# Moving the later wq loads and the last wq-gradient store to Pool's DMA queue, in the backward pass of a decode block with attention over a cache

## The chip, the cores and the metric

The kernel runs on one core of a Trainium2 chip. The metric is the device time of one execution in microseconds (us); lower is better. A core has five engines with instruction streams of their own: PE (matmul), DVE (vector), ACT (scalar), POOL (GpSimd) and SP (which here only issues transfers). SP, ACT and POOL issue the DMA transfers. All transfers are moved by the core's 16 DMA engines; the profile names the queues q1 (issued by SP), q10 (by ACT) and q0 (by POOL, with descriptors made in software).

## The reference, cut to what matters

One token attends with 32 heads over caches of 8192 positions, beside a gated MLP. Wanted are the output and the gradients of all inputs but one. The caches and their gradients are the bulk of the traffic: 32 heads x (K, V, dK, dV) of 2 MiB each.

```python
def _A_ref(x, k_cache, v_cache, wq, wo):
    q = (x @ wq).reshape(B, Sq, Hq, Dh).transpose(0, 2, 1, 3)
    scores = jnp.einsum("bhqd,bhkd->bhqk", q, k) * (Dh ** -0.5)
    p = _softmax(scores, axis=-1)
    o = jnp.einsum("bhqk,bhkd->bhqd", p, v)
    return o.transpose(0, 2, 1, 3).reshape(B, Sq, Hq * Dh) @ wo

x = A_x
xn = _layernorm(x, axis=-1)
return x + _A_ref(xn, A_k_cache, A_v_cache, A_wq, A_wo) + _B_ref(xn, B_w1, B_w3, B_w2)
...
_out, _vjp = jax.vjp(_f, A_x, A_k_cache, A_v_cache, A_wq, A_wo, B_w1, B_w3, B_w2)
_grads = _vjp(grad_out)
```

With one query, dV of a head is the outer product of the probabilities and the gradient of o, dK the outer product of the score gradients and q, and the gradient of wq is the outer product of xn and dq. wq is 640 x 4096 in bf16.

## The kernel before, in words

The order of the instructions on each engine is the order of the program text (a manual schedule). The MLP comes first (some 45 us), then one pass of the loop at L725 per head, then the last head written out from L779.

In a pass, head `h` gets its probabilities (`probs`), its dV in two halves (`outer` with "V"), its score gradients (`dscores`) and its dK in two halves (`outer` with "K"), while the score products of head `h + 1` are made (`product`, L414 on DVE and L416 on PE). `outer` writes into a 2 MiB tile `ot` (L430 on ACT, L436 on DVE) from a pool of four, and after the second half POOL stores it (L443). The last two heads are stored in halves by SP (L441). K tiles come from a pool of three, V tiles from one of two; SP issues their loads (L115 and L122) as soon as a tile is free.

wq is kept in two buffers of 8 heads (`wq_bufs`, 1280 KB each): block `b`, heads `8b` to `8b + 7`, lies in buffer `b % 2`. Blocks 0 and 1 are loaded at the start. When a block's heads are done, ACT writes the block's wq gradient into the same buffer (L372) and POOL stores it (`store_columns`, L141), in columns 0 to 2 and 3 to 4 of the five that each partition holds; `sparing` cuts these stores into 120 and 8 rows, and `turn_lanes` (L137) puts tiny loads into a `lane_pad` between them, which move on the DMA engine at which the next one starts. Only after that may the buffer take block `b + 2`. So just two loads are issued inside the loop, block 2 and block 3, and `WQ_AT` (L718) says where: the key is the head's number within the running block and one of three places in the pass (0 after dV's second half, 1 after the wo load, 2 after dK's second half), the value is the first column, the number of columns and the queue (SP where none is named). Before, ACT loads columns 0 to 2 during the block's third head (heads 10 and 18), and SP one column each at places 0 and 2 of the fourth (heads 11 and 19).

The first reader of block 2 is `prep_steps(4)`, whose first step (the matmuls into `ps_q`, L311) runs in the first `gap` of head 14; for block 3 that is head 22. PE runs it in order, so that all that follows on PE would wait for a late wq.

At the end, the gradient of the last four heads' wq columns is made in the tile `dwq_t` (L802) and stored by ACT (L804); behind it on ACT stands the store of the output (`fin_bf`, L841). SP stores the last wo gradient (L807) and the gradient of x (`dx_bf`, L836). POOL's last transfers are three stores kept back until head 29 (`late`, L767: wq gradient of block 2, a wo gradient, the wq gradient of group 6) and a `lane_pad`.

Of the kernel before, what the change touches and what calls it, by code (L numbers as in the profile page):

```python
# [21 lines left out]
def kernel(  # L22
# [22 lines left out]
    nc = tc.nc  # L45
    H = A_k_cache.shape[1]
    SK = A_k_cache.shape[2]
    DH = A_k_cache.shape[3]
# [7 lines left out]
    GH = 4  # L56
# [36 lines left out]
    dwq_v = out_4.rearrange("(p ci) n -> p ci n", ci=NC)  # L93
# [9 lines left out]
    with tc.manual_schedule(engines=ORDERED):  # L103
# [65 lines left out]
        def load_wq(b, c0=0, n=NC, by=nc.sync.dma_start):  # L169
            wq_g = wq_bufs[b % 2]  # L170
            part, src, _ = wq_part(b, c0, n)
            by(part, src)
            for g in range(b * HB, (b + 1) * HB):
                c0 = (g - b * HB) * GH * DH
                grp.setdefault(g, dict(wq_all=wq_g, wq=wq_g[:, :, c0:c0 + GH * DH]))
# [539 lines left out]
        exps(first)  # L715
        product(first, "DP", 1)
        prev = None
        WQ_AT = {(2, 1): (0, 3, nc.scalar.dma_start), (3, 0): (3, 1), (3, 2): (4, 1)}  # L718

        def wq_columns(h, part):  # L720
            b, r = divmod(h, GW)
            if 0 < b < H // GW - 1 and (r, part) in WQ_AT:
                load_wq(b + 1, *WQ_AT[r, part])

        for h in range(H - 1):  # L725
            n = new_head(h + 1) if h + 1 < H else None
            c = hs.pop(h)
            g, hh = divmod(h, GH)
# [51 lines left out]
        g = c.g  # L780
# [19 lines left out]
        dwq_t = tpool.tile([P, NC, GH * DH], BF16, name="dwq_t", tag="T")  # L800
        for ci in range(NC):
            nc.scalar.activation(dwq_t[:, ci, :], c.G["dqbc"][:].rearrange("p h d -> p (h d)"),  # L802
                                 ACTF.Copy, scale=xn_col[:, ci:ci + 1])
        nc.scalar.dma_start(dwq_v[:, :, g * GH * DH:(g + 1) * GH * DH], dwq_t[:])  # L804
        for r in range(GH):
            nc.vector.tensor_scalar(c.G["wo"][:, r, :], g_bc_bf[:], on[:, r:r + 1], None, ALU.mult)
        nc.sync.dma_start(dwo_v[g], c.G["wo"][:])  # L807
# [64 lines left out]
```

## Time and profile before

| | |
|---|---|
| median of 3 runs | 720.65 us (719.62 to 720.72) |
| the profiled execution | 720.15 us, of it 718.4 us span |
| moved | 303.32 MB, mean 422 GB/s |
| busy | DVE 631.4 us, PE 555.2, ACT 479.3, POOL 49.5 |
| packets q1 / q0 / q10 | 13490 / 10960 / 3196 |
| wq loads inside the loop | ACT at 269.4 and 436.8 us; SP at 286.8, 290.7, 453.8, 456.9 us |
| first use of the new wq blocks (L311) | 351.4 and 516.1 us |
| last store of wq's gradient (L804) | issued at 703.9 us, landed 13.3 us later |

"Span" is the time from the first to the last instruction of the profiled execution. Times in the text are on the span's clock. A DMA's landing is the moment when its semaphore has been counted up by all 16 engines. Not only instructions but every DMA packet (queue, size, start, duration) is in the trace; the queue table of the profile is summed from these.

### The profile page before, as it was taken

How to read it: one execution, taken by the hardware profiler on the slowest of the kernel's cores; microseconds unless marked ns; L12 is line 12 of the kernel's file. 1: busy time of each engine (PE TensorE's matmuls, PEld its weight loads, DVE VectorE, ACT ScalarE, POOL GpSimd, SP SyncE). 2: the span in 40 equal slices, each digit the busy share in tenths (PEclk: the TensorE clock that was granted, in tenths of full speed). 3: DMA queues.
4: the chain of work that ended last, by engine and by line, in shares of the span. 5: the costliest groups of instructions: out<-in, count | busy, mean ns of one | idle time of the engine just before them, and what ended most of it. 6: DMA issues, size and time to landing. Idle time of an engine off the chain costs nothing.

```text
span 718.4 us, 9840 instructions
## 1 busy us (share of the span) xinstructions
PE 555.2 (77%) x3516; PEld 274.3 (38%) x3516; DVE 631.4 (88%) x723; ACT 479.3 (67%) x1456; POOL 49.5 (7%) x91
## 2 busy tenths in 40 slices
PE   5787788888788786775888788497877888888862
PEld 3653343333344333332443344143433334333331
DVE  5789999999999996896799999499999989899992
ACT  2165677696779756695487866469677857678551
POOL 0010000000001210000000110000000000000100
PEclk9699989999998988997799979779899889999995
DMA  8999999999999999999999999999999999999997
GB/s 351 415 426 424 431 430 401 430 429 428 434 428 430 430 425 424 425 427 428 430 426 432 430 427 422 428 428 429 429 429 431 430 428 433 427 430 431 428 422 304
DMA packets 27694, 303.32 MB, mean 422 GB/s; under 512 B 3264, under 2 KB 3974, under 8 KB 9982
## 3 DMA queue, kind: packets, MB, share of 16 engines
q1 hardware_dynamic: 13490, 154.89, 51.0%
q0 software_dynamic: 10960, 137.72, 45.1%
q10 hardware_dynamic: 3196, 10.10, 3.5%
q8 instruction: 27, 0.44, 0.2%
q14 instruction: 21, 0.17, 0.1%
HBM read 151.34 MB, written 151.34 MB: 421 GB/s over the span
## 4 chain that ended last, share of the span: by engine, by line
DVE 41%; DMA 36%; PE 15%; ACT 5%; issue 1%; SPq 0%; POOL 0%; DVEq 0%; ACTq 0%; POOLq 0%
DMA Kt<-in_A_k_cache_dram 20%; DVE T L414 19%; DVE ot L436 12%; DMA out_dram<-ot 10%; DMA lane_pad<-in_A_wq_dram 4%; PE ob L485 4%; PE psDP L416 4%; ACT ot L430 3%; PE psS L416 3%; DMA dbc<-in_B_w_dram 2%; DVE S_sb L457 1%; DVE DP_sb L511 1%; PE ps_od L501 1%; PE dx_ps L612 1%; DVE P L476 1%
## 5 line engine op out<-in xcount | busy, mean ns | idle before, releaser
L416 PE MATMUL psDP<-T,ident_bf 128*128 128x512 bf16 x512 | 158.1, 465 | 67.4 <-DVE T L414 67.2
L416 PEld LDWEIGHTS <-ident_bf 128*128 128x128 bf16 x1024 | 107.9, 109 | 205.3 <-issue 131.1
L430 ACT ACTIVATE ot<-qs_g,Uf 128x128 bf16<-128x128 bf16 x496 | 151.7, 394 | 43.5 <-DVE Uf L523 26.5
L414 DVE TENSOR_TENSOR T<-Kt,qs_g 128x4096 bf16<-128x4096 bf16 x64 | 146.4, 2287 | 14.9 <-DMA Kt<-in_A_k_cache_dram 13.7
L430 ACT ACTIVATE ot<-do_g,Pf 128x128 bf16<-128x128 bf16 x504 | 154.0, 389 | 7.0 <-DMA out_dram<-ot 6.0
L414 DVE TENSOR_TENSOR T<-Vt,do_g 128x4096 bf16<-128x4096 bf16 x64 | 146.0, 2282 | 5.6 <-DMA Vt<-in_A_v_cache_dram 5.6
L416 PE MATMUL psS<-T,ident_bf 128*128 128x512 bf16 x512 | 126.4, 391 | 10.0 <-DVE T L414 10.0
L436 DVE TENSOR_TENSOR ot<-qs_g,U 128x3072 bf16<-128x3072 bf16 (+1 forms) x64 | 113.2, 1768 | 12.4 <-DMA out_dram<-ot 12.3
L436 DVE TENSOR_TENSOR ot<-do_g,P 128x3072 bf16<-128x3072 bf16 (+1 forms) x64 | 112.9, 1764 | 7.1 <-DMA out_dram<-ot 6.1
L443 POOL DMA_DIRECT2D out_dram<-ot x60 | 32.2, 536 | 548.4 <-DVE Uf L523 315.1
L485 PE MATMUL ob<-Vt,P 128*4 128x512 bf16 x512 | 62.2, 386 | 0.0
L485 PE MATMUL ob<-Kt,U 128*4 128x512 bf16 x512 | 60.5, 379 | 1.3 <-DVE U L518 1.3
L478 ACT ACTIVATE Pf<-E,rZ 128x16 f32<-128x16 f32 x32 | 9.7, 304 | 57.9 <-DVE rZ L474 57.9
L542 ACT ACTIVATE dq_diag<-ident_bf,odq 128x128 bf16<-128x128 bf16 x32 | 12.8, 401 | 50.9 <-DVE odq L538 50.9
L501 PEld LDWEIGHTS ps_od<-pick,wide 128*128 128x128 f32 x256 | 42.2, 233 | 8.3 <-issue 2.8
L501 PE MATMUL ps_od<-pick,wide 128*128 128x2 f32 x256 | 37.2, 267 | 0.5 <-ACT wide L493 0.5
L461 PE MATMUL sm<-ident_f,mrow 128*128 128x128 f32 x64 | 15.9, 331 | 24.1 <-DVE mrow L459 24.1
L485 PEld LDWEIGHTS <-U 128*4 128x4 bf16 x512 | 19.8, 84 | 37.4 <-DVE U L518 6.9
L485 PEld LDWEIGHTS <-P 128*4 128x4 bf16 x512 | 20.6, 85 | 24.7 <-issue 1.5
L493 ACT COPY wide<-ob 128x256 f32<-128x256 f32 x64 | 20.0, 362 | 10.5 <-PE ob L485 10.5
L306 ACT COPY woT<-ps_t 128x512 bf16<-128x512 bf16 x40 | 23.0, 576 | 5.2 <-PE ps_t L301 4.5
L457 DVE TENSOR_REDUCE S_sb<-psS 128x64 f32<-128x512 f32 x32 | 21.9, 685 | 4.5 <-PE psS L416 4.5
(173 smaller groups left out, 549.9 us busy)
## 6 DMA issues: line engine op xcount, KB each, us to landing
out_dram<-ot POOLq DMA_DIRECT2D x60, 2048.0 KB, 24.1
Kt<-in_A_k_cache_dram SPq DMA_DIRECT2D x32, 2048.0 KB, 26.5
Vt<-in_A_v_cache_dram SPq DMA_DIRECT2D x32, 2048.0 KB, 20.5
out_dram<-ot SPq DMA_DIRECT2D x8, 1024.0 KB, 13.3
out_dram<-wo_g ACTq DMA_DIRECT2D x6, 640.0 KB, 15.2
wo_g<-in_A_wo_dram ACTq DMA_DIRECT2D x6, 640.0 KB, 15.6
wq<-in_A_wq_dram SPq DMA_DIRECT2D x2, 1280.0 KB, 33.7
w1t<-in_B_w_dram SPq DMA_DIRECT2D x1, 2160.0 KB, 12.7
```

Of the source, the lines that this page charges most:

```text
L306: nc.scalar.copy(woT[:], ps_t[:])
L414: nc.vector.tensor_tensor(T[:], src[:, :, ds_], vec[:, ds_].unsqueeze(1).to_broadcast([P, J, DHH]), ALU.mult)
L416: nc.tensor.matmul(ps[:], lhsT=ident_bf[:], rhs=T[:, :, RUN * i:RUN * (i + 1)], start=(half == 0 and i == 0), stop=(half == 1 and i == DHH ...
L430: nc.scalar.activation(st.ot[half][:, JH - ACT_J + j].rearrange("p a b -> p (a b)"), vec, ACTF.Copy, scale=wf[:, half, j:j + 1])
L436: nc.vector.tensor_tensor(st.ot[half][:, 0:n], vec.rearrange("p (a b) -> p a b", b=2).unsqueeze(1).to_broadcast([P, n, DH // 2, 2]), w2[:, ...
L443: nc.gpsimd.dma_start(dst.rearrange("p j d -> p (j d)"), st.rows[:])
L457: nc.vector.tensor_reduce(st.S[:], st.ps["S"][:], AX.X, ALU.add)
L461: nc.tensor.matmul(st.sm[:, 8:8 + P], lhsT=mrow[:].to_broadcast([P, P]), rhs=ident_f[:], start=True, stop=True, skip_group_check=True)
L485: nc.tensor.matmul(ob[c0:c0 + WIDE, :], lhsT=w2[:, WIDE * q:WIDE * (q + 1), 0], rhs=src[:, WIDE * q:WIDE * (q + 1), :].rearrange("p j d -> ...
L493: nc.scalar.copy(part[:], ob[:, i * (WIDE // 2) * DH:(i + 1) * (WIDE // 2) * DH])
L501: nc.tensor.matmul(st.od, lhsT=st.wide[i][:, b * DH:(b + 1) * DH], rhs=pick[:, r, :], start=(r == 0), stop=(r == WIDE - 1), skip_group_che ...
L542: nc.scalar.activation(dq_diag[:], ident_bf[:], ACTF.Copy, scale=odq[:, 1:2])
```

## The change

Two lines change. The wq loads inside the loop are both issued by POOL, at places 0 and 2 of the block's fourth head (heads 11 and 19): columns 0 to 2 directly behind the store of dV, columns 3 and 4 directly behind the store of dK. The store of `dwq_t` is issued by POOL too.

```diff
-        WQ_AT = {(2, 1): (0, 3, nc.scalar.dma_start), (3, 0): (3, 1), (3, 2): (4, 1)}
+        WQ_AT = {(3, 0): (0, 3, nc.gpsimd.dma_start), (3, 2): (3, 2, nc.gpsimd.dma_start)}
...
-        nc.scalar.dma_start(dwq_v[:, :, g * GH * DH:(g + 1) * GH * DH], dwq_t[:])
+        nc.gpsimd.dma_start(dwq_v[:, :, g * GH * DH:(g + 1) * GH * DH], dwq_t[:])
```

In the built program ACT loses three DMA instructions, SP four, POOL gains five; PE's and DVE's orders stay as they were, and no compute instruction changes. No byte is added or taken away.

## The prediction

> **What bounds the kernel now.** I read the slices first, then the stretches of 18 us, the queue table, DVE's waits, and last the end of the timeline. The page (span, slices, queues) has these lines:
>
> ```profile
> span 718.4 us, 9840 instructions
> ...
> DVE  5789999999999996896799999499999989899992
> ...
> DMA  8999999999999999999999999999999999999997
> GB/s 351 415 426 424 431 430 401 430 429 428 434 428 430 430 425 424 425 427 428 430 426 432 430 427 422 428 428 429 429 429 431 430 428 433 427 430 431 428 422 304
> ...
> q1 hardware_dynamic: 13490, 154.89, 51.0%
> q0 software_dynamic: 10960, 137.72, 45.1%
> q10 hardware_dynamic: 3196, 10.10, 3.5%
> ```
>
> The reader is to see that the DMA engines are full in every slice but the first and the last, while DVE has a hole (the 4 at 450 us). The three queues' shares add up to 99.6%. Four stretches, with their columns (busy us of each engine, granted clock, DMA share, GB/s):
>
> ```profile
> core 0: us, PE busy (x) PEld busy (x) DVE busy (x) ACT busy (x) POOL busy (x), PEclk, DMA share, GB/s
> ...
> 270.00:288.00 18.00, 12.75 (x68) 5.71 (x69) 10.47 (x14) 12.16 (x36) 1.06 (x2) 0.81 1.02 425
> ...
> 324.00:342.00 18.00, 9.84 (x54) 4.65 (x50) 11.74 (x11) 8.27 (x28) 1.06 (x2) 0.75 1.00 424
> ...
> 450.00:468.00 18.00, 7.54 (x52) 3.34 (x52) 8.03 (x9) 8.93 (x28) 0.53 (x1) 0.76 1.01 425
> ...
> 684.00:702.00 18.00, 12.09 (x95) 6.64 (x94) 16.54 (x20) 10.45 (x34) 0.00 (x0) 0.99 1.01 422
> ```
>
> DVE works 8 of 18 us in one of them and the DMA engines carry as much as ever. So a compute stall in the loop is the effect of the full DMA engines, and taking one away moves it elsewhere. What DVE waits for there:
>
> ```profile
> DVE ot L436 <- DMA out_dram<-ot: 18.4, 4, 9.9
> DVE T L414 <- DMA Kt<-in_A_k_cache_dram: 13.7, 10, 3.7
> DVE T L414 <- DMA Vt<-in_A_v_cache_dram: 5.6, 1, 5.6
> ```
>
> Stores that free an `ot` tile too late, then loads. The time is therefore the sum of what the packets cost on the slowest DMA engine, plus a start and an end. The end, from the timeline:
>
> ```profile
> 702.84 0.43 SPq L807 DMA_DIRECT2D out_dram<-wo_g  x1
> ...
> 703.89 0.62 ACTq L804 DMA_DIRECT2D out_dram<-dwq_t  x1
> ...
> 708.10 0.33 SPq L836 DMA_DIRECT2D out_dram<-dx_bf  x1
> 708.29 0.30 ACTq L841 DMA_DIRECT2D out_dram<-fin_bf  x1
> ```
>
> By the trace's landing records, POOL's kept-back stores are drained at 708.9, the wo gradient lands at 716.6, `dwq_t` at 717.2 (its first engine at 710.7, the middle one at 714.8), `dx_bf` at 717.0 and `fin_bf`, behind `dwq_t` on q10, at 717.4. DMA engines with work in hand, not the 708.3 of the last issue, set the end.
>
> **The change, part by part.** *Price of the packets.* In the packet records SP's and ACT's wq loads are packets of 2 KB at 86.6 ns mean: 2 blocks x 128 rows x 5 columns = 1280 packets, 110.8 us, over 16 engines 6.93 us. POOL's stores of the same buffers were packets of 4 KB: q0 holds 1112 of them at 160.0 ns, and 1112 x 4 KB is the 4480 KB of wq gradient that POOL stores, all but 32 KB. If POOL's loads are packed alike, they are 640 x 160.0 ns / 16 = 6.40 us: -0.53. `dwq_t` by ACT is 640 packets of 1 KB at 46.1 ns, 1.84 us; by POOL 160 x 160.0 / 16 = 1.60: -0.24. No row shows POOL loading wq, so the bounds: 2 KB packets that stay so, 0; the dearest row per KB (46.1 ns for 1 KB), 2560 KB x 46.1 / 16 = 7.37, +0.44. I take -0.53, since the nearest rows, the stores of the same tiles by the same queue, are packed.
>
> *Issue.* A POOL DMA takes 0.54 us (60 `ot` stores), up to 1.02 for 640 pieces (the last L767). Five more are 4 us on an engine busy 49.5 of 718: nothing on the path. Behind each stands only the next store; the dK store of head 11 follows its neighbour by 9.4 us. ACT loses a 4.2 us wait ahead of its load at 269.4 (L172's semaphore instruction, 4157 ns), in a stretch where DVE waits for stores anyway: 0.
>
> *Waits of the loads.* In the built program a POOL DMA waits for the landing of the eighth before it. For block 2 these are head 9's dV store (landed 279.5) and the 120-row gradient store (283.3); the loads' places are behind the stores at 286.6 and 296.0. For block 3: 445.7 and 453.7 against 452.8 and 469.7. All over before: 0. If the cover were gone, the next dK store would wait with them, and four `ot` tiles later DVE.
>
> *Who is delayed now.* On one engine q0 and q1 take turns packet by packet: between 256.5 and 259.5 us q0 moved 71 packets of 4 KB beside 61 of 16 KB on q1. The Trainium skill (DMA: Bandwidth & Descriptors, "Queues, rings and completion order") has the engines switch only after a whole packet of some 9 to 17 descriptors; by the 71 to 61 the trace does not agree for these 16 KB rows. By the rule each of POOL's 20 small packets of a block would stand behind a row block of 8 x 0.611 us, 20 x (0.160 + 4.9) = 101 us from 286.6 and 452.8, so that L311 would wait 36 and 38 us and the time come near 790; the rows leave it a chance of 0.01.
>
> By turns of single packets SP's 2 KB packets cost the loads turns: 8 per engine and part, 16 x (0.087 + 0.611 of a 16 KB store packet) = 11.2 us per block; DVE's 5.6 us wait for V at 329 and the 3.7 for K at 343 follow. After, 12 + 8 packets of 4 KB cost the stores 20 x (0.160 + 0.611) = 15.4 us per block, and what is late next is an `ot` tile two heads on. The DMA engines stay full meanwhile, since loads run ahead: 0 on the path. That cover ends if compute is more than 5.0 us later at the end: `dwq_t` is issued at 703.9 and q0 drains at 708.9.
>
> *Landing of wq.* Before, head 11's dK store landed at 321.0 and head 19's at 493.8. With the first part's 12 turns (9.3 us) and the second's 8 (6.2) on top, wq lands near 336 and 509; L311 needs it at 351.4 and 516.1. Hidden, with 15 and 7 us; without the cover PE waits, and DVE behind it.
>
> *End.* `dwq_t` comes into q0 behind 708.9 on the last engine, its 10 packets among SP's last; `fin_bf` is alone on q10. The last landing goes from 717.4 to between that and `dx_bf`'s 717.0: -0.4 to 0, I take -0.2.
>
> Sum: -0.53 - 0.24 - 0.2 = -0.97. The profiled execution, 718.4 span and 1.75 around it, would go from 720.15 to 719.2. It was 0.5 below the median, so I forecast 719.7.
>
> **The rivals.** *Stores too late (slower).* The 15.4 us fall on the stores, and four `ot` tiles cover less than K's and V's five. For it: the stretch at 450 us, where POOL's small gradient packets had just this effect (the 9.9 us wait). Against it: such a wait cost no DMA time there. It decides when the lateness outlives the ten heads behind head 19; a second wait of 9.9 us, less the 5.0 of cover, gives +4.9: 720.65 + 4.9 - 0.8 for the packets = 724.8; with half of the lateness forgotten by then, 722.3.
>
> *More than the packets (faster).* The engines finish 6.5 us apart (710.7 to 717.2, the middle at 714.8). If the lag comes from the hardware queues' small pieces, moving them levels it: up to -2.4 beside the -0.97, 717.3. For it: no other row explains the lag. Against: both queues spread 128 rows over the engines evenly.
>
> *The transfer is hidden anyway (no change).* POOL's loads stay at 2 KB and the end is SP's: 0, 720.65. The Trainium skill (the same page, "Issuing engines are not separate DMA queues") says that spreading issues only saves issue time; by that rule this is the outcome. Against: the 4 KB rows.
>
> **How the numbers follow.** Forecast 0.55, own range 718.4 to 721.2 (the packets' bounds and the 1.1 us between the three runs); stores too late 0.20; levelled 0.13; no change 0.11; the skill's long packets 0.01. The range 717.4 to 723.0 leaves out most of the worst half of the slow case and the tail of the levelled one. Faster or slower means by over 0.2% (1.44 us), about what a measurement of this kernel can tell: the forecast puts 0.18 of its 0.55 below 719.2 and 0.02 above 722.1; with 0.13 of levelling, faster is 0.31. The slow case gives 0.17 of its 0.20, with the 0.02 and the 0.01 slower is 0.20; the rest, 0.49, is no change that can be told.
>
> **What would show it.** q10 falls from 10.10 to 7.9 MB, q0 rises to 141, and q0's packets by 800 and 16 semaphore writes for each of five transfers, some 880 and not 2000. DVE's waits for K and V at 329 to 347 shrink, and waits for `ot` appear at heads 13 and 21. L311 does not start late. The DMA share stays at 1.00 to 1.02 from 270 to 700. I am wrong if a stretch after 290 falls below 0.98, if L804 lands last, or if the time leaves 718.4 to 721.2.

## The result, and the profile after

The changed kernel takes 722.38 us (median of 20 runs, 719.56 to 725.3), the kernel before beside it 719.74 (20 runs, 719.05 to 721.71): a ratio of 1.0027, interval 1.0017 to 1.0038. It is slower by 0.27%, some 1.9 us. The ratio on record isn't the quotient of the two medians, which lie 2.64 us apart (1.0037); where this text gives microseconds from medians, the ratio beside them is the safer number. The time lies in the range of 717.4 to 723.0; the forecast said 719.7 and gave most weight to no change that can be told, so the direction was missed. The profiled execution took 722.25 us.

The page after (span, slices, queues):

```profile
span 720.5 us, 9824 instructions
...
GB/s 358 409 422 428 431 429 428 431 429 429 428 432 429 426 427 424 420 424 425 432 428 429 429 426 424 422 419 429 430 426 431 426 431 428 429 432 428 429 421 260
...
q1 hardware_dynamic: 12914, 153.84, 50.5%
q0 software_dynamic: 11840, 141.00, 46.2%
q10 hardware_dynamic: 1740, 7.87, 2.6%
```

The queues moved as foretold: q0 has 880 packets more. Of DVE's waits:

```profile
DVE ot L436 <- DMA out_dram<-ot: 35.2, 8, 7.7
DVE T L414 <- DMA Kt<-in_A_k_cache_dram: 6.2, 7, 1.7
```

K's waits fell from 13.7 to 6.2 us, V's are gone, those for `ot` rose from 18.4 to 35.2. The swap was foretold. What was not is seen in the stretches beside the wq loads (columns as before the prediction). Before:

```profile
288.00:306.00 18.00, 13.66 (x94) 6.12 (x93) 16.75 (x18) 11.93 (x42) 0.53 (x1) 0.91 1.01 427
306.00:324.00 18.00, 14.19 (x80) 6.50 (x80) 17.42 (x20) 16.59 (x47) 1.06 (x2) 0.91 1.01 425
...
468.00:486.00 18.00, 17.36 (x102) 8.14 (x101) 16.63 (x20) 11.12 (x35) 1.07 (x2) 0.77 1.01 430
```

After:

```profile
288.00:306.00 18.00, 15.95 (x106) 7.25 (x104) 16.85 (x20) 11.94 (x40) 1.28 (x2) 0.91 1.01 421
306.00:324.00 18.00, 13.28 (x86) 6.35 (x85) 17.75 (x19) 16.72 (x49) 1.09 (x2) 1.00 1.01 421
...
468.00:486.00 18.00, 13.65 (x102) 6.59 (x100) 17.75 (x18) 14.90 (x47) 1.09 (x2) 1.00 1.00 417
```

The share of the DMA engines (the last column but one) is 1.00 to 1.01 in all six, and yet 4 to 13 GB/s are missing after. A share counts how long packets are under way; it doesn't say that they are as short as they could be.

The packet records give the account. For packets that start between 265 and 650 us (before the first changed load and up to the loop's last heads), summed and divided by the 16 engines:

| us | before | after | difference |
|---|---|---|---|
| small packets (2 to 8 KB) | 24.17 | 23.76 | -0.41 |
| 16 KB packets, what they took above 611.3 ns each | 1.65 | 3.16 | +1.51 |
| tiny packets and semaphore writes | 1.16 | 1.04 | -0.12 |
| less overlap of packets | 3.40 | 3.04 | +0.36 |
| sum | | | +1.34 |

611.3 ns is what nearly every 16 KB packet takes. "Less overlap" is the time by which the packets of all engines together exceed 385 us per engine: packets of one engine overlap a little, and after they do so less. The bytes agree: 164.90 MB before and 164.32 after in the same stretch, 0.58 MB or 1.36 us at 428 GB/s. Of the 1.51 us of long packets 1.34 lie where the wq loads are (265 to 335 and 440 to 545 us), with packets of up to 1253 ns in the first of these stretches and 1886 in the second (before 1258 and 1144). The saving in small packets was right; it is paid for more than three times over by the large packets around them.

The other part is the end. The timeline after:

```profile
708.33 0.86 POOL L804 DMA_DIRECT2D out_dram<-dwq_t  x1 [37.04 <-issue]
...
710.64 0.33 SPq L836 DMA_DIRECT2D out_dram<-dx_bf  x1
710.83 0.29 ACTq L841 DMA_DIRECT2D out_dram<-fin_bf  x1
```

In this execution `dwq_t` left 4.4 us later than before: 2.2 because ACT's last write of it came later (706.08; the granted clock was 0.72 from 684 to 702 us, 0.99 before), and 2.2 between that write and POOL's issue. The last landings were 718.58 (`dwq_t`), 718.99 (the wo gradient) and 719.16 (`dx_bf`), against 717.4 before. The two profiled executions don't show the loop's loss in their spans: the one after had 0.5 MB (1.2 us) of lead at 265 us, ahead of all that was changed, and none at 650. By the bytes moved, what their spans differ by arose after 650 us.

### The profile page after: what moved, and what is told of

Read it like the earlier page. It is cut to its first block, busy times and chain, and to the rows that moved or that the text cites. A ratio compares the mean times of both kernels' runs of the same rounds, so it can differ in the third digit from the quotient of the medians.

```text
span 720.5 us, 9824 instructions
## 1 busy us (share of the span) xinstructions
PE 552.0 (77%) x3516; PEld 271.6 (38%) x3516; DVE 632.0 (88%) x723; ACT 479.2 (67%) x1456; POOL 53.5 (7%) x96
## 3 DMA queue, kind: packets, MB, share of 16 engines
q10 hardware_dynamic: 1740, 7.87, 2.6%
## 4 chain that ended last, share of the span: by engine, by line
DVE 39%; DMA 35%; PE 18%; ACT 5%; issue 2%; SPq 0%; DVEq 0%; ACTq 0%
DMA out_dram<-ot 22%; DVE T L414 19%; DMA Kt<-in_A_k_cache_dram 11%; DVE ot L436 11%; PE ob L485 5%; PE psDP L416 4%; ACT ot L430 3%; PE psS L416 3%; DMA dbc<-in_B_w_dram 2%; DVE S_sb L457 2%; DVE DP_sb L511 1%; PE ps_od L501 1%; ACT woT L306 1%; PE ps_d L324 1%; PE dx_ps L612 1%
## 5 line engine op out<-in xcount | busy, mean ns | idle before, releaser
L416 PE MATMUL psDP<-T,ident_bf 128*128 128x512 bf16 x512 | 151.6, 449 | 61.4 <-DVE T L414 61.4
L416 PEld LDWEIGHTS <-ident_bf 128*128 128x128 bf16 x1024 | 106.2, 107 | 193.7 <-issue 116.5
L430 ACT ACTIVATE ot<-do_g,Pf 128x128 bf16<-128x128 bf16 x504 | 153.9, 389 | 19.8 <-DMA out_dram<-ot 18.9
L416 PE MATMUL psS<-T,ident_bf 128*128 128x512 bf16 x512 | 123.8, 386 | 8.7 <-DVE T L414 8.7
L485 PE MATMUL ob<-Vt,P 128*4 128x512 bf16 x512 | 67.1, 408 | 0.0
L542 ACT ACTIVATE dq_diag<-ident_bf,odq 128x128 bf16<-128x128 bf16 x32 | 12.9, 402 | 52.1 <-DVE odq L538 52.1
L501 PEld LDWEIGHTS ps_od<-pick,wide 128*128 128x128 f32 x256 | 39.7, 221 | 8.1 <-issue 2.5
L501 PE MATMUL ps_od<-pick,wide 128*128 128x2 f32 x256 | 35.1, 259 | 0.5 <-ACT wide L493 0.5
L485 PEld LDWEIGHTS <-U 128*4 128x4 bf16 x512 | 19.8, 84 | 36.6 <-DVE U L518 6.9
L301 PE MATMUL ps_t<-ident_bf,wo_g 128*128 128x128 bf16 x160 | 16.7, 231 | 16.2 <-ACT dqbc_g L553 15.0
L461 PEld LDWEIGHTS sm<-ident_f,mrow 128*128 128x128 f32 x64 | 9.9, 194 | 45.9 <-DVE mrow L459 40.4
```

The lines of the kernel that those rows point to most:

```text
L301: nc.tensor.transpose(ps_t[:, hh * DH:(hh + 1) * DH], wo_g[:, hh, ci * P:(ci + 1) * P], ident_bf[:])
L416: nc.tensor.matmul(ps[:], lhsT=ident_bf[:], rhs=T[:, :, RUN * i:RUN * (i + 1)], start=(half == 0 and i == 0), stop=(half == 1 and i == DHH ...
L430: nc.scalar.activation(st.ot[half][:, JH - ACT_J + j].rearrange("p a b -> p (a b)"), vec, ACTF.Copy, scale=wf[:, half, j:j + 1])
L461: nc.tensor.matmul(st.sm[:, 8:8 + P], lhsT=mrow[:].to_broadcast([P, P]), rhs=ident_f[:], start=True, stop=True, skip_group_check=True)
L485: nc.tensor.matmul(ob[c0:c0 + WIDE, :], lhsT=w2[:, WIDE * q:WIDE * (q + 1), 0], rhs=src[:, WIDE * q:WIDE * (q + 1), :].rearrange("p j d -> ...
L501: nc.tensor.matmul(st.od, lhsT=st.wide[i][:, b * DH:(b + 1) * DH], rhs=pick[:, r, :], start=(r == 0), stop=(r == WIDE - 1), skip_group_che ...
```

## The experiments

Every experiment is the kernel before with the edit shown, so that each stands against the kernel before. In the table "MB" is what was moved from 265 to 650 us, "long" the time of 16 KB packets above 611.3 ns there, "dry" how long q0 and q1 had no packet of 1 KB or more there (pauses over 1.2 us), all from one profiled execution each.

| kernel | moved | ratio and interval | MB | long, us | dry q0 / q1, us |
|---|---|---|---|---|---|
| before | | 1 | 164.90 | 1.65 | 0 / 12.4 |
| e2 | store only | 1.0025 [1.0015, 1.0035] | 165.00 | 1.44 | 0 / 12.9 |
| e5 | out_0 by POOL | 1.0036 [1.0024, 1.0048] | 165.03 | 1.42 | 0 / 12.7 |
| e6 | a late store cut | 1.0052 [1.0038, 1.0066] | 164.97 | 1.42 | 0 / 11.3 |
| e7 | the same, other lane | 1.0031 [1.0018, 1.0043] | 164.67 | 2.05 | 3.4 / 13.7 |
| e14 | columns 3, 4 to POOL | 1.0001 [0.999, 1.0012] | 164.94 | 1.58 | 0 / 30.8 |
| e15 | V loads later | 1.0008 [0.9999, 1.0018] | 164.87 | 1.70 | 3.6 / 15.0 |
| after | loads and store | 1.0027 [1.0017, 1.0038] | 164.32 | 3.16 | 0 / 41.2 |
| e1 | loads to POOL | 1.0017 [1.0007, 1.0028] | 164.46 | 2.91 | 0 / 43.3 |
| e11 | the same, store by SP | 1.0015 [1.0001, 1.0029] | 164.60 | 2.48 | 0 / 41.4 |
| e3 | both parts by SP, later | 1.0056 [1.004, 1.0071] | 163.38 | 4.52 | 27.7 / 20.3 |
| e4 | both parts by ACT, later | 1.0024 [1.0009, 1.0039] | 164.11 | 2.96 | 0 / 28.9 |
| e8 | loads cut | 1.012 [1.0106, 1.0135] | 161.33 | 8.74 | 0 / 50.2 |
| e9 | four parts, POOL | 1.004 [1.0024, 1.0055] | 164.18 | 3.40 | 0 / 44.3 |
| e10 | old places, POOL | 1.0039 [1.0024, 1.0054] | 164.53 | 2.30 | 0 / 35.6 |
| e12 | POOL and SP | 1.0025 [1.0014, 1.0036] | 164.22 | 2.48 | 0 / 22.5 |
| e13 | columns 0 to 2 to POOL, later | 1.0014 [1.0003, 1.0025] | 164.60 | 2.31 | 0 / 15.3 |
| e16 | columns 0 to 2 later, ACT | 1.0025 [1.0009, 1.0042] | 163.67 | 3.69 | 7.1 / 17.8 |
| e17 | columns 0 to 2 to POOL, old place | 1.003 [1.0014, 1.0047] | 164.25 | 3.13 | 0 / 19.8 |
| e18 | columns 0 to 2 to SP, old place | 1.0106 [1.0068, 1.0143] | 162.61 | 6.07 | 16.5 / 0 |

The upper seven keep columns 0 to 2 of wq as they were, the lower thirteen move them. Long packets take 1.42 to 2.05 us in the upper and 2.30 to 8.74 in the lower ones. Within the lower ones the ratio doesn't follow them run by run (e10 has 2.30 us and 1.0039, e13 2.31 us and 1.0014): the last three columns are of one execution, the ratio is of 4 to 20, and e2, e5, e6 and e7 lose their time at the end.

**The two parts apart, and other queues.** e1 has only the changed loads, e2 only the changed store; e3 and e4 issue the same two parts at the same places by SP and by ACT.

```diff
 # e1                    e3: (3, 0): (0, 3), (3, 2): (3, 2)       e4: nc.scalar.dma_start
+        WQ_AT = {(3, 0): (0, 3, nc.gpsimd.dma_start), (3, 2): (3, 2, nc.gpsimd.dma_start)}
 # e2
+        nc.gpsimd.dma_start(dwq_v[:, :, g * GH * DH:(g + 1) * GH * DH], dwq_t[:])
```

> Only the two wq loads go to POOL; the last wq gradient is stored by ACT as before. If the small packets ahead of the stores in q0 are the cause (theory L), the ratio to the kernel before is 1.002 to 1.004, the dK and dV stores of heads 20 to 29 land on their last engine 5 us or more after the middle one (before 3.4 to 4.4 us), and the end is at 719.5 us or later. If the late store of dwq_t is the cause (theory S), the ratio is 0.998 to 1.001. If the low TensorE clock at the end of the profiled execution was (theory C), the ratio is 0.999 to 1.001 as well, and so is that of the next kernel.

> Only the store of dwq_t goes to POOL; the wq loads stay as before. Theory S: POOL issues it some 2 us after ACT is done (2.24 us in the changed kernel, against 0.28 us for most of its stores), it lands last, ratio 1.002 to 1.004. Theory L: ratio 0.999 to 1.001, the landing lag of heads 20 to 29 as before (3.4 to 4.4 us).

> The wq loads at the changed kernel's two places, in the same two parts, but issued by SP; dwq_t by ACT. It parts the queue from the place: if theory L is about POOL's queue, the ratio is 0.999 to 1.001 and K and V wait (5 us or more); if about later loading or larger parts whatever the queue, 1.002 or more.

> The same two parts at the same two places, issued by ACT, so in a queue of their own in front of nobody; dwq_t by ACT. Theory L: 0.998 to 1.001, and neither the loads of K and V nor the stores are put off. Theory C: no difference from the kernel before in any of the four.

Medians against 719.86: e1 721.13, e2 721.99, e3 724.02, e4 722.34. Both parts cost by themselves, 1.3 and 2.1 us, and together 2.6; by the ratios it is 1.2, 1.8 and 1.9 us, with intervals too wide to tell whether the whole is less than the sum. Loads in the fourth head cost on each queue. The clock isn't the cause: averaged over the runs it was 0.890 in e1 and e2, 0.892 in the kernel before beside them and 0.892 in the changed kernel. In e2 the loop is unharmed (165.00 MB), and the landings are late by half a microsecond only: the last is `dx_bf`'s at 717.92 (`dwq_t` 717.34), against 717.4, yet the span is 721.6. What lies behind is not a transfer. In the instruction records POOL has a closing DRAIN, which in e2 ends 3.44 us behind the landing of POOL's last transfer:

| us | last landing on POOL's queue | DRAIN ends | between |
|---|---|---|---|
| before | 709.43 | 712.84 | 3.40 |
| e1 | 710.88 | 714.45 | 3.57 |
| e2 | 717.34 | 720.78 | 3.44 |
| e5 | 716.44 | 719.89 | 3.44 |
| after | 718.58 | 718.96 | 0.38 |

Before, POOL's queue is empty some 8 us ahead of the others and the DRAIN is over in time. In e2, with `dwq_t` on POOL, it sets the end. In the profiled execution of the changed kernel it was short and did not.

**The DRAIN alone.** To tell it from a late store, e5 leaves `dwq_t` to ACT and gives POOL the last and smallest store, 1.3 KB of output. e6 and e7 test another thought, that one lagging DMA engine sets the end: they cut POOL's kept-back store of block 2's wq gradient into 120 and 8 rows, with the lane_pads at lane 4 and at lane 8. e8 cuts the wq loads in that manner.

```diff
 # e5
+        nc.gpsimd.dma_start(out_0.rearrange("a b (c p) -> (a b c) p", p=P), fin_bf[:])
 # e6                                       e7: by=lambda d, s: sparing(d, s, 8)
+                    store(dst, part, True, by=sparing)
 # e8
+        WQ_AT = {(3, 0): (0, 3, sparing), (3, 2): (3, 2, sparing)}
```

> The kernel before, with only the last store, 1.3 KB of the output, issued by POOL in place of ACT. Theory D: POOL's closing DRAIN (L867) ends 3.4 us after the landing of POOL's last transfer (3.40 to 3.57 us in five of the six traces so far, 0.38 in the sixth), which was hidden while that transfer landed at 709 us. Then the DRAIN ends near 720.5, last of all, and the ratio is 1.002 to 1.004 though no wq byte has moved. Theory S (the 640 KB of dwq_t behind q0's backlog are what costs): ratio 0.999 to 1.001.

> The kernel before, with the kept-back store of block 2's wq gradient (1280 KB, L767) cut as sparing() cuts the others, so that the fifth DMA engine gets 20 packets of 4 KB fewer. Theory I: one engine has more to do than the others and sets the end (last landing 2.6 us behind the middle engine's), and it is the one that sparing() spares: the end comes 1 to 2 us earlier, ratio 0.997 to 0.999. Rival: the lag belongs to no fixed engine, ratio 0.9995 to 1.001.

> As the kernel before it, but the ninth engine is spared. Theory I: the lagging engine gets no relief and some packets more (0.2 us): ratio 1.000 to 1.002, and at least 0.001 above the kernel before it. Rival: no difference between the two.

> Both wq loads on POOL at the changed kernel's places, each cut by sparing(); dwq_t by ACT. Theory I (the loads on POOL cost 1.2 us because one engine falls further behind): the lag of q0's last engine behind the middle one in heads 20 to 29 falls from 4.7 to 7.6 us to below 4, ratio 0.998 to 1.0005. Theory L (small packets ahead of the stores cost, whichever engine has them): 1.0015 or more.

Medians against 720.06: e5 722.55, e6 723.58, e7 722.52, e8 728.74. A store of 1.3 KB costs 2.5 us where POOL issues it. In e5 SP's waits at the end, and the span:

```profile
span 720.7 us, 9824 instructions
...
SPq L867 <- DMA out_dram<-fin_bf: 6.1, 1, 6.1
...
SPq L867 <- PEq L867: 2.9, 2, 2.4
```

Before:

```profile
SPq L867 <- PEq L867: 0.7, 2, 0.5
```

The last line of each is the closing barrier, which every engine must reach; the profile names PE's sequencer, but the instruction that lets SP go is POOL's (720.01 in e5), just behind the DRAIN. SP's waits for the landings end at 717.4; then it waits 2.4 us, until the DRAIN has ended (719.89), and the span closes 0.8 us later. Sparing an engine helps nowhere. In e6 and e7 some 1.5 and 1.2 MB are lost from 680 to 702 us (322 to 378 GB/s in stretches of 6 us from 684 on); why cut stores are so slow there was not settled.

**Is it the burst, the amount or the drain?** e9 spreads the loads over four parts, e10 has POOL issue the three parts at the places of the kernel before, e11 is the changed kernel with `dwq_t` by SP, and e12 puts columns 3 and 4 on SP behind POOL's columns 0 to 2.

```diff
 # e9, with g = nc.gpsimd.dma_start
+        WQ_AT = {(2, 2): (0, 1, g), (3, 0): (1, 1, g), (3, 2): (2, 1, g), (4, 0): (3, 2, g)}
 # e10
+        WQ_AT = {(2, 1): (0, 3, g), (3, 0): (3, 1, g), (3, 2): (4, 1, g)}
 # e11
+        WQ_AT = {(3, 0): (0, 3, g), (3, 2): (3, 2, g)}
+        nc.sync.dma_start(dwq_v[:, :, g * GH * DH:(g + 1) * GH * DH], dwq_t[:])
 # e12
+        WQ_AT = {(3, 0): (0, 3, g), (3, 1): (3, 2)}
```

> Four parts on POOL (1, 1, 1 and 2 columns) from head 10's dK store to head 12's dV store, dwq_t by ACT as before. Theory B (the bursts): 12 and 8 small packets in a row on each engine throw q0 back at once, a queue runs dry later and the other alone carries less. Parts of 4 packets avoid it: 164.7 to 165.0 MB moved between 265 and 650 us, as wherever the loop is unchanged, ratio 0.9985 to 1.0010. Rival A (the amount): what counts is that 20 small packets per engine stand in q0, however they are spaced: 164.3 to 164.6 MB, ratio 1.0010 to 1.0028, like the loads on POOL in two parts.

> The three parts and places of the kernel before (columns 0 to 2 in the third head, one column at each of two places of the fourth), all on POOL, dwq_t by ACT as before. Theory B (the bursts): the 12 packets of the first part still come in a row, so something of the loss stays: 164.4 to 164.7 MB between 265 and 650 us, ratio 1.0005 to 1.0020. Rival P (the place: it is the later start, in the fourth head, that lets a queue run dry): 164.8 to 165.0 MB, ratio 0.9985 to 1.0008. Rival A (the amount on q0): 164.3 to 164.5, ratio 1.0010 to 1.0028.

> The changed kernel with dwq_t stored by SP instead of POOL. Theory D (POOL's closing DRAIN, some 3.4 us behind its last landing): POOL's last transfer is again the lane_pad near 671 us, its DRAIN ends by 717 and is hidden; the ratio is that of the loads alone, 1.0008 to 1.0025, below the changed kernel's 1.0027 by up to 1 us. Rival (the DRAIN costs nothing beside the loads, as in the one profiled execution of the changed kernel): 1.0020 to 1.0038.

> Columns 0 to 2 on POOL behind head 11's dV store as in the change, columns 3 and 4 on SP just behind them, dwq_t by ACT as before. Measure: the time that the 16 KB packets between 265 and 650 us take above 611.3 ns each, summed over 16 engines; 1.4 to 2.1 us wherever the loop is unchanged, 2.3 to 4.5 with the loads moved (8.7 where they were cut). Theory U (uneven queues: all small packets in one queue set it back against the other, and the 16 KB packets lengthen while the two are out of step): with 12 packets in q0 and 16 in q1 both are set back alike, so 1.4 to 2.1 us and a ratio of 0.9985 to 1.0010. Rival N (any load placed in the fourth head costs this, in whatever queue): 2.3 to 4.5 us and a ratio of 1.0012 or more.

The burst fell: spread parts cost no less (1.0040, 3.40 us of long packets), though in e9 the PE also waits 5.3 us for wq at L311. The place alone fell with e10, uneven queues with e12. e11's DRAIN ended at 713.14, hidden, and its ratio of 1.0015 is that of the loads alone; its interval doesn't exclude the changed kernel's 1.0027, so what the DRAIN costs in the changed kernel itself isn't shown; that it costs stands on e2 and e5.

**Which part of the loads.** By then it was seen that q1 has nothing to move for 20 to 50 us where the loads are moved, against 11 to 14 us, and the next theory was that this costs. e13 moves only ACT's part to POOL (and, since a place takes one load, SP's column 3 from place 0 to 1), e14 only SP's; e15 leaves wq alone and delays five V loads.

```diff
 # e13
+        WQ_AT = {(3, 0): (0, 3, nc.gpsimd.dma_start), (3, 1): (3, 1), (3, 2): (4, 1)}
 # e14
+        WQ_AT = {(2, 1): (0, 3, nc.scalar.dma_start), (3, 0): (3, 2, nc.gpsimd.dma_start)}
 # e15
+            if h + 2 < H and h not in (14, 16, 22, 24, 26):
                 load_v(h + 2)
...
+            if h in (14, 16, 22, 24, 26):
+                load_v(h + 2)
             blocks_sum(c)
```

> Only ACT's part (columns 0 to 2) goes to POOL in the fourth head; columns 3 and 4 stay two loads of SP (place 1 and 2), dwq_t by ACT as before. Theory R (the load queue q1 running dry is what costs: its restarts and the stretches with one queue alone lengthen 16 KB packets): q1 keeps SP's 16 small packets and is dry for 20 us or less between 265 and 650 us; 16 KB packets' time above 611.3 ns 1.4 to 2.1 us and ratio 0.9985 to 1.0012, if it is SP's part that keeps q1 busy. Rival N (12 small packets in a row in q0 cost this by themselves): 2.3 us or more, ratio 1.0012 to 1.0030.

> Only SP's part (columns 3 and 4) goes to POOL behind head 11's dV store; columns 0 to 2 stay with ACT in the third head, dwq_t by ACT as before. Theory R: q1 has lost its small packets and is dry for over 20 us; 16 KB packets' time above 611.3 ns 2.3 us or more, ratio 1.0010 to 1.0030. Rival N (what costs is the burst of 12 in q0; here it has only 8): 1.4 to 2.1 us, ratio 0.9985 to 1.0010.

> All wq loads as before; the V loads of five heads (16, 18, 24, 26, 28) are issued some 10 us later in the pass, so that q1 runs dry there for longer. Theory R: q1 dry for 30 us or more between 265 and 650 us, 16 KB packets' time above 611.3 ns 2.3 us or more, ratio 1.0012 or more. Rival N (a dry queue costs nothing as long as the stores fill the engines; the small packets cost): 1.4 to 2.1 us, ratio 0.9985 to 1.0010.

The theory fell, and the part was found. In e14 q1 is dry for 30.8 us and nothing is lost (1.0001, 719.84 us against 720.15); in e13 it is dry for 15.3 and the ratio is 1.0014. e15 didn't make q1 much drier (15.0 us), so it decides nothing. Eight small packets per engine and block in front of q0's stores are free here; moving columns 0 to 2 is what costs (e13's 1.0014 beside 1.0017 for both parts in e1).

**Queue or place.** For these columns e16 changes the place and e17 the queue, e18 takes the old place on SP. In e16, as in e13, SP's column 3 moves from place 0 to 1 as well (in e16 SP's two loads are issued 1.8 us later than before).

```diff
 # e16
+        WQ_AT = {(3, 0): (0, 3, nc.scalar.dma_start), (3, 1): (3, 1), (3, 2): (4, 1)}
 # e17
+        WQ_AT = {(2, 1): (0, 3, nc.gpsimd.dma_start), (3, 0): (3, 1), (3, 2): (4, 1)}
 # e18
+        WQ_AT = {(2, 1): (0, 3), (3, 0): (3, 1), (3, 2): (4, 1)}
```

> Columns 0 to 2 still loaded by ACT, but in the fourth head (place 0); SP's two columns at places 1 and 2, dwq_t by ACT as before. Theory Q (the queue: in q0 the 12 small packets stand in front of each engine's next stores, in q10 they go beside them): 16 KB packets' time above 611.3 ns 1.4 to 2.1 us between 265 and 650 us, ratio 0.9985 to 1.0010. Rival P (the place: later by some 17 us, the load falls together with SP's part and another phase of the loop): 2.3 us or more, ratio 1.0012 to 1.0030.

> Columns 0 to 2 loaded by POOL instead of ACT at the place of the kernel before (third head, place 1); SP's part and dwq_t as before. Theory Q: 16 KB packets' time above 611.3 ns 2.3 us or more, ratio 1.0012 to 1.0040. Rival P: 1.4 to 2.1 us, ratio 0.9985 to 1.0010.

> Columns 0 to 2 loaded by SP instead of ACT at the place of the kernel before (third head, place 1); the rest as before. Theory G (a gap to fill: the small packets are free where they move while the load queue has nothing else): SP's queue q1 moves them from some 272 to 290 us, when it would be empty; 16 KB packets' time above 611.3 ns 1.4 to 2.1 us between 265 and 650 us, ratio 0.9985 to 1.0010. Rival T (a third queue is what makes them cheap): 2.3 us or more, ratio 1.0012 to 1.0040.

With e13 this is a square: ACT early 1, ACT late 1.0025, POOL early 1.0030, POOL late 1.0014. Each change alone costs, so neither theory holds by itself; the three intervals overlap, so which costs most isn't shown. The packets say where they went. Before, columns 0 to 2 of block 2 move on q10 from 273.0 to 288.3 us, and q1 is empty from 280.7 to 289.7: a good half of them take turns with stores alone. In e16 they move from 286.8 to 309.5, seven tenths of them after q1 has started again (291.7). In e17 they stand behind POOL's stores: of the last 192 packets of 4 KB on q0, as many as these columns make, 141 start after 292.6, when q1 has started again, the last at 300.9. In e16 the loss can be seen on its own, here against the same stretch before. e16:

```profile
354.00:366.00 12.00, 10.68 (x68) 4.72 (x67) 11.90 (x13) 9.84 (x33) 0.53 (x1) 0.91 0.93 354
```

Before:

```profile
354.00:366.00 12.00, 10.20 (x77) 5.24 (x72) 11.90 (x14) 8.39 (x28) 1.06 (x2) 1.00 1.01 434
```

80 GB/s over 12 us are 0.96 MB, 2.2 us. There q0 was empty from 357.9 to 365.0: DVE had waited for K at 322 (5.5 us), for V at 339 (4.6) and for K at 351 (4.1), together 14.2 us where before it waited 9.3, and so the next store was issued only at 360.8. A lateness of some 50 us earlier comes back as a store queue with nothing in it; here the cover of loads that run ahead did end.

e18 was to use the same gap by another queue. It failed: 1.0106. On q1 the small packets start at 271.6, but they stand in front of the next K, which was issued 3.2 us later (SP had waited for the buffer) and landed at 298.9 instead of 282.1. DVE then waits for K where it waited for stores:

```profile
DVE T L414 <- DMA Kt<-in_A_k_cache_dram: 45.0, 18, 8.0
DVE ot L436 <- DMA out_dram<-ot: 5.4, 3, 2.8
```

and q0 runs empty in its turn (16.5 us in all). The stretch of 18 us with the lowest rate holds a pause of 2.8 us:

```profile
522.00:540.00 18.00, 14.78 (x87) 7.13 (x88) 17.57 (x19) 12.55 (x41) 1.06 (x2) 0.83 0.97 390
```

So an empty q1 isn't enough: the small packets must not stand in front of large ones either. Nor is it always needed, since in e14 block 2's columns 0 to 2 move from 270.7 to 292.6 beside a q1 with one pause of 3.3 us (282.1 to 285.4) between 265.9 and 304.4, and nothing is lost. What the runs with an unharmed loop have in common is q10, on which nothing large stands behind these columns, together with the third head; but in all of them these columns are loaded as before, so what it is in this pair that spares them isn't shown. No version beat the kernel before; e14 equals it.

## Why the prediction missed

*Price of the packets: right for the loads, too good for the store.* POOL's loads are 640 packets of 4 KB at 160.9 ns. Small packets fell by 0.41 us between 265 and 650 (forecast -0.53), q0 has the 880 packets more, q10 7.87 MB. The -0.24 for `dwq_t` hardly came: its 160 packets of 4 KB took 182 ns each at the end of the changed kernel, 1.82 us against the 1.84 that ACT's 640 took (1.71 in e2).

*Issue, waits, landing of wq: right.* POOL was busy for 53.5 us instead of 49.5. The parts landed at 322.65 and 339.12, 493.3 and 509.8 us (336 and 509 foretold); L311 ran at 346.1 and 516.7 with no wait for wq among PE's. The turns of single packets behind these sums hold: the 71 to 61 (the records have 63) is a count over all 16 engines, but these landings fit it, and not the long turns of the rival.

*Who is delayed: the first failed step.* The prediction put the lateness on the stores, which was right (`ot` waits 35.2 us), and priced it at nothing: "The DMA engines stay full meanwhile, since loads run ahead: 0 on the path." They stay full by their share, and lose 1.51 us by longer 16 KB packets in the profiled execution. Measured by themselves (e1) the loads cost 1.3 us, 1.0017. The test named for it ("a stretch after 290 falls below 0.98") was the wrong one: the share held at 1.00 and GB/s fell to 417. The 5.0 us of cover counted only lateness at the end, not throughput in the loop. The rival of stores too late had the direction and the place; its price was a wait of DVE, where the loss found here is in the packets.

*Rival of no change.* The Trainium skill (DMA: Bandwidth & Descriptors, "Issuing engines are not separate DMA queues") says that starting DMAs from several engines only saves time on the sequencers that issue them. By that, e17 would equal the kernel before; it took 1.0030 [1.0014, 1.0047] with the same bytes at the same place in the program (POOL moves them in packets of 4 KB, ACT in packets of 2 KB), and e18, where SP moves them in packets of 2 KB too, 1.0106. The trace doesn't agree for this kernel: which queue holds a packet decides what stands behind it.

*End: the second failed step, a term left out.* "I take -0.2" looked only at landings. POOL's DRAIN was not in the sum: e2 shows +2.1 us for this store (1.0025) and e5 +2.5 for 1.3 KB (1.0036). "If L804 lands last" was not what happened (`dx_bf` did, at 719.16); that test wouldn't have found it either, as in e2 and e5 the DRAIN comes after all landings. In the profiled execution of the changed kernel it ended at 718.96, 0.38 us behind `dwq_t`'s landing and ahead of `dx_bf`'s, so there SP's last wait, for `dx_bf`, set the end; in how many of the other runs the DRAIN did isn't known.

*Levelled engines: not seen.* In the landing of `dwq_t` the last engine is 4.1 us behind the middle one after, 2.4 before.

*The sum.* Loads +1.3 (e1) and store +2.1 (e2) stand beside 2.6 together. A later end of the transfers and a later DRAIN may overlap in part; the intervals don't settle it. The forecast had -0.8 for the two packet terms, -0.2 for the end and 0 for the rest.

What stays open: why 16 KB packets lengthen when the queues get out of step. They do it at the start of a load on an empty queue (in the kernel before at 107.5 to 114.7 us, with q1 packets of up to 1992 ns), but the restart at 289.7 us in the same trace shows none of it. In the changed kernel 0.83 of the 3.16 us start within 4 us behind four restarts of q1, in e14 only 0.05 of 1.58 behind four restarts that look alike. The 20 programs are the same up to 265 us, and yet by then their traces had moved 110.64 to 112.11 MB, up to 3.4 us apart, with such a dip near 108 us in some: the runs of one kernel spread by as much (2.7 us before, 5.7 after).

## What to carry to other kernels

Where transfers set the time, read GB/s beside the DMA share, and sum the packets' durations above their usual one: a full share can hide a loss. Before a transfer in small packets is moved to another queue or place, look at what will stand behind it there, and try its parts one by one: here one part was free and the other cost about as much as both. Be wary of giving POOL the last store of a kernel: here its closing DRAIN mostly ended some 3.4 us behind its last landing, and cost nothing only where it was over before the other queues finished.

## What the runs showed of the hardware

- POOL's closing DRAIN ended 3.40 to 3.73 us behind the last landing of POOL's queue in 18 of 20 traces, but only 0.38 (after) and 0.71 us (e8) in two; what decides that was not found.
- A 16 KB packet takes 611 ns beside another queue and alone, but up to 1992 ns at one start of a queue in the kernel before (107.5 us) at a DMA share of 0.99, and up to 1785 in e16 from 358.5 to 365 us at 0.93 over its stretch.
- POOL's issue of `dwq_t` came 2.24 us after its data was written in the changed kernel, and 0.28 us after it in e2, with the same kept-back stores still in POOL's queue both times; why isn't known.
